# Last attention sums, turned rows' tile, first w_sp loads and the difference's stores: other queues, pools and places in a transformer block

## The chip, the cores and the metric

One core of a Trainium2 chip. A core has five engines with instruction streams of their own: TensorE (PE; matmuls, PEld its weight loads), VectorE (DVE), ScalarE (ACT), GpSimd (POOL) and SyncE (SP, which here only issues DMAs). They meet through semaphores. The metric is the device time of one execution in microseconds (us), lower is better; "the time" is the median of three runs.

## The reference

A transformer block in fp32 on x of 2048 rows by 512:

```
h   = x + wo · MHA(LN(x))                 32 heads of 16, softmax over 2048 keys
z   = gelu(LN(h) · w_in)                  2048 x 1376, halves z1 and z2 of 688
g   = w_sp · LN(z2) + b_sp                w_sp is 2048 x 2048: it mixes rows
out = h + (z1 * g) · w_out
```

## The kernel before

All products of w_in, wo, w_sp and w_out are made in three parts (mm3, L109 to L111): each fp32 operand is split into a high and a low part, and high·high, high·low and low·high are summed in PSUM. A split is one ScalarE copy (high, L101) and one VectorE subtraction (low, L106); for w_sp's blocks the lines are L989 and L990.

Three stages matter here.

**Attention** (up to about 1352 us). Per group of heads and block of 512 queries, scores, exponentials and products with v, and a `gather` (L760ff.): ScalarE and VectorE copy the result from PSUM to the tile `o`; then for each of four heads SyncE stores the head's rows to `o_scr` (L775) and its sums of exponentials into the tile `sums` (L776). `more_h` makes the first three rows' h between the last units, normalizes and turns them (`flip`, which returns `write`: four DMAs to `ht_scr`, L667).

**Row blocks** (1354 to 1520 us; the loop that starts with `for k in range(NB)`). Sixteen blocks of 128 rows, in the order 0, 1, 2, 8, 9, 10, 3, 11, ... 15; "row k" is the k-th of them. For row k, TensorE makes h of row k+3 (L642, 12 matmuls; none from k = 13 on) and the products of w_in with the row's turned block, in three chunks of 12 matmuls (four chunks of 344 columns for row 15). ScalarE does the gelu of each chunk (L1054) and, after the first chunk, splits `o` of row k+4 and `ht`, the turned block of row k+1 (`split_turned`). VectorE takes statistics of the second half of z (L1114 to L692); ScalarE normalizes it (L1066) and stores both halves to `z_scr` from its own DMA queue (L1061, L1067). Then `meanwhile` issues on SyncE: the fetch of row k+2's turned block (`fetch_turned`, L675), loads for row k+6, and the writes of row k+3's turned block. From row 8 of the loop on, the two halves of the rows meet (rows k and k-8 by number) and VectorE or GpSimd forms t1, t2, t3 and n4 of them.

Also here the first blocks of w_sp are fetched and combined: the w_sp product is made by a scheme of fewer block products, which needs `a22`, `s3` (a difference, L1009), `s2` and others. At the end of rows 11 and 12 `ask` loads a21, a22 and a11 (two DMAs of 256 KB each, L995); in row 13 GpSimd makes the six operations of `difference` and `sums`, and `sums` stores the difference to `s_scr` (two DMAs, L1031). In row 14 s3 is split, at its end s2, behind row 15 a22.

**The g products** (from 1520 us): products of w_sp's blocks, 48 matmuls each, the first two with s3 (with t3) and a22 (with n4), in two pools of PSUM banks; then the rest up to the output.

In the second and third stage the order on all five engines is that of the program text (`manual_schedule`). PSUM has eight banks. The w_in products rotate through seven of them (`mid_ps`), and h's product has the eighth. Each DMA of SyncE or ScalarE signals through one of eight completion semaphores (DMAHW0 to DMAHW7), taken in rotation by both; an issue waits until the transfer that used its semaphore before has landed. Tiles lie where pools are opened; a pool opened after another was closed lies on its memory, and then the first write waits for the last readers of the old tiles. The z tiles (`mid_2`) lie, among others, on attention's last `o` tile.

Of the kernel before, what the change touches and what calls it, by code (L numbers as in the profile page):

```python
# [22 lines left out]
DH = 16  # L23
# [37 lines left out]
def block_kernel(ctx: ExitStack, tc: tile.TileContext, x, wqkv, wo, w_in, w_sp4, b_sp, w_out, out):  # L61
# [648 lines left out]
    with ExitStack() as at:  # L710
# [49 lines left out]
        def gather(hg, qb, pool=sm):  # L760

            o = pp.tile([P, 512], F32, name="o", bufs=1)
            if pool is sm and not later:
                nc.scalar.activation(o, pv[0], AF.Copy)
            else:
                nc.vector.tensor_copy(o[:, :256], pv[0][:, :256])
                if later and pool is sm:
                    nc.vector.tensor_copy(o[:, 256:], pv[0][:, 256:])
                else:
                    nc.scalar.activation(o[:, 256:], pv[0][:, 256:], AF.Copy)  # L770
            cols = slice(qb * 512, (qb + 1) * 512)
            sums = pool.tile([P, 16], F32, name="sums")
            for j in range(4):
                h = head(hg, j % 2, j // 2)
                nc.sync.dma_start(o_scr[h * DH:(h + 1) * DH, cols], o[32 * j:32 * j + DH, :])  # L775
                nc.sync.dma_start(sums[32 * j:32 * j + 32, :], o[32 * j + DH:32 * j + VW, :])  # L776
            sums_[0] = (hg, cols, sums, pool)

        def by_age(place):
# [113 lines left out]
        def more_h(k):  # L893

            for _ in range(k):
                if not pieces:
                    sb = h_rows[made[0] // (3 * DB)]
                    acc = later[0].tile([P, 512], F32, name="h")
                    pieces.extend([sb, acc, h_products(sb, acc)])
                sb, acc, products = pieces  # L900
                next(products)
                made[0] += 1
                if made[0] % (3 * DB):
                    continue
                pieces.clear()
                if made[0] == 6 * DB:
                    split_turned(h_rows[0])
                after = h_rows[made[0] // (3 * DB)]
                o = os_.pop(after)
                hi, lo = o2s[after] = [e2.tile([P, DB, P], F32R, name=f"o2{i}", bufs=1) for i in range(2)]  # L910
                nc.vector.tensor_copy(hi, o)
                add_h(sb, acc, lambda: nc.vector.tensor_sub(lo, o, hi.bitcast(F32)))
                mv, rs = scale_h(sb)
                hn = e2.tile([P, D], F32, name="hn", bufs=3)
                nc.vector.tensor_scalar(hn, xrs.pop(sb), mv[:, 0:1], rs,
                                        op0=ALU.subtract, op1=ALU.mult)
                flip(sb, hn)()

        made = [0]
        units = [(hg, qb, kb) for hg in range(HG) for qb in range(NQ) for kb in range(NB)]  # L920
        turn, later = [0], []
# [2 lines left out]
        with tc.manual_schedule(engines={E.PE, E.Activation, E.DVE, E.SP}):  # L924
            end = len(units) - 2 * LEAD
            for n in range(0, end, 2):
                hg, qb, kb = units[n]
                if hg + 1 < HG and n % 64 < 24 and n % 4 == 0:
                    load_k(hg + 1, [n % 64 // 4])
                if hg + 1 < HG and n % 64 < 12 and n % 4 == 2:  # L930
                    load_d(hg + 1, [n % 64 // 4])
                if hg + 1 < HG and n % 64 == 30:
                    load_v(hg + 1)
                if kb == 2 and n // NB + 3 < HG * NQ:
                    load_q(n // NB + 3)
                place = n % NB // 2
                while m < min(8 * HG * NQ, n // 2 + LEAD + 1 + (not place and n > 0)):
                    for kind, some in max_pair(m, True).items():
                        steps_of[kind].extend(some)
                    m += 1  # L940
                if place or not n:
                    if place != 1 or n == 2:
                        play(START if not n else BEFORE if n + 2 == end else LAST if place == 7 else ORDER, units[n:n + 2])
                else:
                    play(FIRST_TWO, units[n:n + 4])
                if kb == 6 and sums_:
                    invert()
                if n % 32 == 16 and n < 6 * 32:
                    load_weights(n // 32)
                if n in (476, 482):  # L950
                    load_o(h_rows[(476, 482).index(n)])
                if n == 482:
                    split_o(h_rows[0], "pool", "pool")
            load_o(h_rows[2])
            hT.append(wc.tile([P, 2, 2, DB, P], F32R, name="hT", tag="w2"))
            maxima.close()
            for stack in reversed(singles):
                stack.close()
            doubles.extend(at.enter_context(tc.tile_pool(name=f"ps_d{i}", bufs=1, space=PSUM)) for i in range(2))
            later.append(attn.enter_context(tc.tile_pool(name="ps_l", bufs=1, space=PSUM, side="right")))  # L960
            play_final(units[end:])
    attn.close()


# [24 lines left out]
            nc.scalar.activation(hi, src, AF.Copy)  # L989
        (nc.gpsimd if el == "pool" else nc.vector).tensor_sub(lo, src, hi.bitcast(F32))  # L990

    def load_a(halves, i, j, p):

        for n, t in enumerate(halves):
            nc.sync.dma_start(t, w_sp4[p + HB * i][:, HB * j + QB * n:HB * j + QB * n + QB, :])  # L995

    def cut(t):
        return [t[:, QB * n:QB * n + QB, :] for n in range(2)]
# [12 lines left out]
    def half(name, tag, bufs=2, pool=None):  # L1011
        return [(pool or e2).tile([P, QB, P], F32, name=name, tag=tag, bufs=bufs) for _ in range(2)]

    def ask(i, j, p, tag, pool=None):

        t = half(f"a{i}{j}", tag, 3 if tag in ("xr", "hn") else 2, pool)
        load_a(t, i, j, p)
        return t

    def difference(a11, a21, e=nc.vector):  # L1020
# [5 lines left out]
    def sums(p, a11, a21, a22, e=nc.vector):  # L1026

        combine(e, a21, a21, a22, ALU.add)
        combine(e, a11, a21, a11, ALU.subtract)
        for n in range(2):  # L1030
            nc.sync.dma_start(cut(s_scr[p])[n], a11[n])  # L1031

    ctx.enter_context(tc.manual_schedule(engines={E.PE, E.Activation, E.DVE, E.Pool, E.SP}))
    with ExitStack() as mid:
        m2 = mid.enter_context(tc.tile_pool(name="mid_2", bufs=2))
        zs, zst = {}, {}
        ph = mid.enter_context(tc.tile_pool(name="mid_ph", bufs=1, space=PSUM))
        ps = mid.enter_context(tc.tile_pool(name="mid_ps", bufs=7, space=PSUM))

        def new_z(sb):  # L1040
            zs[sb] = [m2.tile([P, FH], F32, name=f"z{i}", bufs=1 + 4 * i) for i in range(2)]
# [49 lines left out]
        for k in range(NB):  # L1091
# [5 lines left out]
                nb = minus_mean(e2, mv, rs)  # L1097
            if k == NB - 3:
                s3 = difference(a11, a21, nc.gpsimd)
                sums(0, a11, a21, a22, nc.gpsimd)  # L1100
            if k == NB - 2:
                ops = {"s3": put(w[0], s3)}
            if k == NB - 1:
# [18 lines left out]

            def meanwhile():
                if k + 2 < NB:
                    fetch_turned(row[k + 2], m2)
                if k + 6 < NB:
                    load_o(row[k + 6])
                if new is not None:
                    write()

            gate_z(sb, meanwhile)
            if not k:
                invert()
            if k == NB - 5:
                a21, a22 = ask(1, 0, 0, "rc"), ask(1, 1, 0, "o")
            if k == NB - 4:
                a11 = ask(0, 0, 0, "xr")
            if k == NB - 2:
                ops["s2"] = put(w[1], a11)
        ops["a22"] = put(w[2], a22)  # L1140
# [3 lines left out]
    with ExitStack() as fin:  # L1144
# [41 lines left out]
        for p in range(HB):  # L1186
# [18 lines left out]
            if not last:  # L1205
# [7 lines left out]
                nxt["s3"] = put(new[0], difference(a11, a21))  # L1213
                if not p:
                    close67()
                sums(p + 1, a11, a21, a22)
                nxt["s2"] = put(new[1], a11)
            else:
                a11 = put(f[0], a11)
# [269 lines left out]
```

## Time and profile before

| what | us |
|---|---|
| median of three runs | 1810.49 (1808.0 to 1813.44) |
| profiled execution | 1808.73 |
| its span | 1807.0 |
| TensorE busy | 1789.6 |
| VectorE, ScalarE, GpSimd busy | 1519.9, 1376.2, 222.3 |

A row of a timeline reads: start, duration, engine, line, operation, out<-in, shape, count, and in brackets the idle time of the engine before it with what ended it. A row of the waits reads: who waited for whom, then total, number and longest. A row of the chain reads: start, duration, what. "SPq" and "ACTq" are DMA issues on SyncE's and ScalarE's queue.

### The profile page before, as it was taken

To read this page: it belongs to the slowest core of one execution; us is meant where nothing else is said; L and a number is where in the kernel's file an instruction comes from. 1 tells how busy PE (TensorE), PEld (TensorE's weight loads), DVE (VectorE), ACT (ScalarE), POOL (GpSimd) and SP (SyncE) were. 2 spreads that over 40 slices of the span, in tenths; PEclk is the share of its full clock that TensorE was granted. 3 is DMA by queue.
4 is the path that set the end of the run, shared out by engine and by line. 5 is a ranking of instruction groups with operands and counts; after the bars stand their busy time and mean duration, and the time that the engine had idled before them with its cause. 6 is when DMAs were issued, how large, how long until landed. Compare 5 with 4: busy or idle time off the path is not lost.

```text
span 1807.0 us, 35997 instructions
## 1 busy us (share of the span) xinstructions
PE 1789.6 (99%) x13307; PEld 1046.6 (58%) x13307; DVE 1519.9 (84%) x3051; ACT 1376.2 (76%) x2673; POOL 222.3 (12%) x299
## 2 busy tenths in 40 slices
PE   9999999999999999999999999999999998999999
PEld 6876444444444444444444444444448887999998
DVE  6487999999999999999999999999847886778664
ACT  3224999999999999999999999999984444334231
POOL 2241000011010100000000000000100863001111
PEclk9999999999999999999999999999999999999999
DMA  5687211221131121122022121110247775668562
GB/s 197 180 197 191 45 28 34 48 58 35 39 61 33 42 44 28 24 58 34 17 50 37 26 40 36 28 21 15 63 103 196 218 205 161 215 203 278 185 196 92
DMA packets 251608, 169.86 MB, mean 94 GB/s; under 512 B 158264, under 2 KB 196680, under 8 KB 250088
## 3 DMA queue, kind: packets, MB, share of 16 engines
q1 hardware_dynamic: 246648, 156.15, 33.9%
q10 hardware_dynamic: 4752, 11.41, 1.7%
q8 instruction: 105, 1.72, 0.4%
q14 instruction: 71, 0.58, 0.1%
q0 software_dynamic: 32, 0.01, 0.0%
HBM read 103.88 MB, written 62.69 MB: 92 GB/s over the span
## 4 chain that ended last, share of the span: by engine, by line
PE 97%; DMA 1%; DVE 1%; SPq 0%; ACT 0%; POOL 0%; issue 0%; ACTq 0%; DVEq 0%; POOLq 0%
PE pv L754 30%; PE s L728 11%; PE s L238 9%; PE m L728 9%; PE m L238 7%; PE acc L109 5%; PE acc L111 5%; PE acc L110 5%; PE g L111 4%; PE g L110 4%; PE g L109 4%; PE acc L642 2%; PE tp L1349 1%; PE h L642 1%; PE acc L1370 0%; PE tp L392 0%
## 5 line engine op out<-in xcount | busy, mean ns | idle before, releaser
L732 ACT ACTIVATE pt<-s 128x512 f32<-128x512 f32 (+1 forms) x1149 | 668.7, 633 | 3.3 <-PE s L728 1.7
L754 PE MATMUL pv<-pt,vst 128*32 128x256 f32 (+1 forms) x6048 | 595.2, 467 | 0.0
L243 DVE TENSOR_REDUCE mx<-s 128x1 f32<-128x512 f32 x826 | 540.4, 684 | 42.1 <-PE s L238 33.9
L732 ACT ACTIVATE pt<-m 128x512 f32<-128x512 f32 x855 | 500.6, 616 | 0.2 <-PE m L728 0.2
L243 DVE TENSOR_REDUCE mx<-m 128x1 f32<-128x512 f32 x682 | 453.0, 683 | 28.2 <-PE m L238 22.5
L728 PE MATMUL s<-qst,kst 50*128 50x512 f32 x1193 | 418.6, 438 | 0.0
L238 PE MATMUL s<-kst,qst 48*128 48x512 f32 x963 | 343.9, 422 | 0.0
L728 PE MATMUL m<-qst,kst 50*128 50x512 f32 x855 | 340.1, 440 | 0.0
L238 PE MATMUL m<-kst,qst 48*128 48x512 f32 x794 | 291.2, 423 | 0.0
L728 PEld LDWEIGHTS s<-qst,kst 50*128 50x128 f32 x1193 | 187.6, 184 | 144.9 <-DVE mx L243 91.0
L754 PEld LDWEIGHTS pv<-pt,vst 128*32 128x32 f32 x6048 | 120.5, 108 | 217.2 <-issue 208.1
L728 PEld LDWEIGHTS m<-qst,kst 50*128 50x128 f32 x855 | 146.4, 184 | 129.4 <-DVE mx L243 88.9
L238 PEld LDWEIGHTS s<-kst,qst 48*128 48x128 f32 x963 | 166.9, 185 | 40.3 <-issue 12.8
L238 PEld LDWEIGHTS m<-kst,qst 48*128 48x128 f32 x794 | 137.2, 185 | 41.6 <-issue 15.5
L103 POOL CAST mparts<-nm 128x16 fp32r<-128x16 f32 x32 | 6.3, 196 | 865.5 <-DVE nm L256 865.5
L248 ACT ACTIVATE ab<-s 128x512 f32<-128x512 f32 x167 | 100.3, 601 | 14.2
L252 DVE CUSTOM_DVE_ANT_0 ab<-s,ab 128x512 f32<-128x512 f32 x137 | 93.5, 683 | 5.1 <-PE s L238 5.1
L989 ACT ACTIVATE ws<-a 128x512 fp32r<-128x512 f32 x80 | 45.7, 620 | 48.7 <-PE g L111 23.8
L252 DVE CUSTOM_DVE_ANT_0 ab<-m,ab 128x512 f32<-128x512 f32 x112 | 76.5, 683 | 4.8 <-PE m L238 4.8
L109 PE MATMUL acc<-wi,hT 128*128 128x464 f32 (+2 forms) x196 | 72.7, 371 | 7.2 <-ACT hT L101 7.2
L238 PE MATMUL s<-dst,qst 48*128 48x512 f32 x167 | 79.7, 477 | 0.0
L111 PE MATMUL acc<-wi,hT 128*128 128x464 f32 (+2 forms) x196 | 72.8, 371 | 0.0
(219 smaller groups left out, 2554.6 us busy)
## 6 DMA issues: line engine op xcount, KB each, us to landing
a<-in_w_sp SPq DMA_DIRECT2D x80, 256.0 KB
qst<-q_scr SPq DMA_DIRECT2D x192, 64.0 KB
z_scr<-z ACTq DMA_DIRECT2D x32, 344.0 KB
kst<-k_scr SPq DMA_DIRECT2D x42, 256.0 KB
k_scr<-part SPq DMA_DIRECT2D x16, 512.0 KB
q_scr<-part SPq DMA_DIRECT2D x16, 512.0 KB
z<-z_scr SPq DMA_DIRECT2D x14, 344.0 KB
b<-z_scr SPq DMA_DIRECT2D x24, 172.0 KB
```

The costliest lines, as they stand in the source:

```text
L109: nc.tensor.matmul(ps, lh, rh, start=first, stop=False)
L110: nc.tensor.matmul(ps, lh, rl, start=False, stop=False)
L111: nc.tensor.matmul(ps, ll, rh, start=False, stop=last)
L238: nc.tensor.matmul(acc, q[r, p, c], keys[r, p], start=True, stop=True)
L243: nc.vector.reduce_max(at(t, e if t else e - 1), acc, axis=AX.X)
L248: nc.scalar.activation(ab[0], acc, AF.Relu)
L252: nc.vector.tensor_tensor_reduce(ab[0], acc, ab[0], 1.0, LOW, ALU.add, ALU.max, at(0, 0))
L642: yield nc.tensor.matmul(acc, o2[b][:, d, :], wo2[a][:, d, :], start=i == 0, stop=i == 3 * DB - 1)
L728: nc.tensor.matmul(out, kst[hg % 2][r, p, kb * P:(kb + 1) * P], qst[hg * NQ + qb][r, p, :], start=True, stop=True)
L732: nc.scalar.activation(out, scores, AF.Exp, scale=DH ** -0.5)
L754: nc.tensor.matmul(pv[0][32 * j:32 * j + 32, cols], vst[hg % 2][:, c:c + 32], pt[:, places[t, p], cols], start=kb == 0, stop=kb == NB - 1 ...
L989: nc.scalar.activation(hi, src, AF.Copy)
```

## The change

Five edits. The last `gather` loads its sums from ScalarE's queue. The third row's turned block is written behind the last gather's stores (`writes`). Turned blocks have a pool of their own, `mid_3`, in place of `mid_2`. a21, a22 and a11 of the first product are loaded from ScalarE's queue. The stores of the difference to `s_scr` are issued at the end of row 13's `meanwhile`, behind the fetch of row 15's block. And `mid_ps` has five banks, on the right side of PSUM.

```diff
@@ gather
                 nc.sync.dma_start(o_scr[h * DH:(h + 1) * DH, cols], o[32 * j:32 * j + DH, :])
-                nc.sync.dma_start(sums[32 * j:32 * j + 32, :], o[32 * j + DH:32 * j + VW, :])
+                e = nc.scalar if pool is not sm else nc.sync
+                e.dma_start(sums[32 * j:32 * j + 32, :], o[32 * j + DH:32 * j + VW, :])
@@ more_h
-                flip(sb, hn)()
-
+                writes.append(flip(sb, hn))
+                if made[0] < 9 * DB:
+                    writes.pop()()
+
+        writes = []
...
             play_final(units[end:])
+            writes.pop()()
@@ load_a, ask
-    def load_a(halves, i, j, p):
+    def load_a(halves, i, j, p, e=nc.sync):
         for n, t in enumerate(halves):
-            nc.sync.dma_start(t, w_sp4[p + HB * i][:, HB * j + QB * n:HB * j + QB * n + QB, :])
+            e.dma_start(t, w_sp4[p + HB * i][:, HB * j + QB * n:HB * j + QB * n + QB, :])
...
-    def ask(i, j, p, tag, pool=None):
+    def ask(i, j, p, tag, pool=None, e=nc.sync):
         t = half(f"a{i}{j}", tag, 3 if tag in ("xr", "hn") else 2, pool)
-        load_a(t, i, j, p)
+        load_a(t, i, j, p, e)
@@ sums
-        for n in range(2):
-            nc.sync.dma_start(cut(s_scr[p])[n], a11[n])
+
+        def store():
+            for n in range(2):
+                nc.sync.dma_start(cut(s_scr[p])[n], a11[n])
+
+        return store
@@ the row blocks
-        ps = mid.enter_context(tc.tile_pool(name="mid_ps", bufs=7, space=PSUM))
+        ps = mid.enter_context(tc.tile_pool(name="mid_ps", bufs=5, space=PSUM, side="right"))
+        m3 = mid.enter_context(tc.tile_pool(name="mid_3", bufs=2))
...
-                sums(0, a11, a21, a22, nc.gpsimd)
+                store_s2 = sums(0, a11, a21, a22, nc.gpsimd)
...
-                    fetch_turned(row[k + 2], m2)
+                    fetch_turned(row[k + 2], m3)
                 if k + 6 < NB:
                     load_o(row[k + 6])
                 if new is not None:
                     write()
+                if k == NB - 3:
+                    store_s2()
...
-                a21, a22 = ask(1, 0, 0, "rc"), ask(1, 1, 0, "o")
+                a21, a22 = ask(1, 0, 0, "rc", e=nc.scalar), ask(1, 1, 0, "o", e=nc.scalar)
             if k == NB - 4:
-                a11 = ask(0, 0, 0, "xr")
+                a11 = ask(0, 0, 0, "xr", e=nc.scalar)
@@ the later products
-                sums(p + 1, a11, a21, a22)
+                sums(p + 1, a11, a21, a22)()
```

Three places of the instruction order. Lines of the changed program are numbered a few higher (L1054 is L1064, L995 is L1000, L1031 is L1038). In brackets stands what an instruction waits for, by semaphore: an engine's, or a DMA's.

ScalarE, from attention's last copy of `o` to row block 0, before:

```order
L770 ACTIVATE o<-pv 128x256 [waits DMAHW4_49,DMAHW3_49,DMAHW5_49,DMAHW2_49,DMAHW6_49,DMAHW1_49,DMAHW7_49,DMAHW0_49,DVE_49]
L1054 ACT_TABLE_LOAD [waits DMAHW3_49,DMAHW4_49,DMAHW2_49,DMAHW5_49,DMAHW1_49,DMAHW6_49,DMAHW0_49,DMAHW7_49,PE_49]
L1054 ACTIVATE z_19146<-acc 128x464 [waits Activation_49]
L101 ACTIVATE o_19162<-o 128x512 [waits Pool_49]
L101 ACTIVATE hT<-ht 128x512
```

and in the change:

```order
L770 ACTIVATE o<-pv 128x256 [waits DMAHW4_49,DMAHW3_49,DMAHW5_49,DMAHW2_49,DMAHW6_49,DMAHW1_49,DMAHW7_49,DMAHW0_49,DVE_49]
L777 DMA sums<-o 32x1x16 [waits DMAHW4_49,Activation_49,Pool_49]
L777 DMA sums<-o 32x1x16 [waits DMAHW6_49]
L777 DMA sums<-o 32x1x16 [waits DMAHW0_49]
L777 DMA sums<-o 32x1x16 [waits DMAHW1_49]
L1064 ACT_TABLE_LOAD
L1064 ACTIVATE z_19149<-acc 128x464 [waits PE_49]
L101 ACTIVATE o_19165<-o 128x512 [waits Pool_49]
L101 ACTIVATE hT<-ht 128x512 [waits DMAHW7_49]
```

The four loads of the sums stand between the copy and the first gelu's table load, and that load no longer waits for DMAs.

SyncE, from row 11's end to row 13's (`a` are blocks of w_sp, `hz` a turned row), before:

```order
L995 DMA a_20685<-in_w_sp 128x512 [waits DMAHW6_49]
L995 DMA a_20686<-in_w_sp 128x512 [waits DMAHW7_49,Activation_49]
L654 DMA h_scr<-xr 128x512 [waits DMAHW0_49,DVE_49]
L675 DMA ht<-ht_scr 128x4x128 [waits DMAHW2_49,DMAHW1_49,Activation_49]
L667 DMA ht_scr<-hz 32x16x32 [waits DVE_49]
L667 DMA ht_scr<-hz 32x16x32 [waits DMAHW3_49]
L667 DMA ht_scr<-hz 32x16x32 [waits DMAHW4_49]
L667 DMA ht_scr<-hz 32x16x32 [waits DMAHW6_49]
L995 DMA a_20803<-in_w_sp 128x512 [waits DMAHW7_49]
L995 DMA a_20804<-in_w_sp 128x512 [waits DMAHW1_49,Activation_49]
L1031 DMA s_scr<-a_20803 128x512 [waits DMAHW2_49,Pool_49]
L1031 DMA s_scr<-a_20804 128x512 [waits DMAHW3_49,Pool_49]
```

The next row there is the fetch of row 15's block. In the change:

```order
L654 DMA h_scr<-xr 128x512 [waits DMAHW7_49,DVE_49]
L675 DMA ht<-ht_scr 128x4x128 [waits DMAHW4_49,DMAHW2_49,DMAHW5_49,DMAHW0_49,Activation_49]
L667 DMA ht_scr<-hz 32x16x32 [waits DVE_49]
L667 DMA ht_scr<-hz 32x16x32
L667 DMA ht_scr<-hz 32x16x32 [waits DMAHW6_49]
L667 DMA ht_scr<-hz 32x16x32 [waits DMAHW0_49]
L675 DMA ht<-ht_scr 128x4x128 [waits DMAHW4_49,DMAHW2_49,DMAHW6_49,DMAHW0_49,Activation_49]
L1038 DMA s_scr<-a_20806 128x512 [waits DMAHW3_49,Pool_49]
L1038 DMA s_scr<-a_20807 128x512 [waits Pool_49]
```

The fetch of row 15's block follows its own four writes, and the two stores stand behind it.

ScalarE, from row 12's last gelu to row 13's second, in the change:

```order
L1064 ACTIVATE z_20726<-acc 128x464 [waits PE_49]
L1071 DMA z_scr<-z_20726 128x688 [waits DMAHW6_49,Activation_49]
L1076 ACTIVATE z_20727<-z_20727,nb,rs_r_20794 128x688 [waits DVE_49]
L1077 DMA z_scr<-z_20727 128x688 [waits DMAHW1_49,Activation_49]
L1000 DMA a_20806<-in_w_sp 128x512 [waits DMAHW3_49]
L1000 DMA a_20807<-in_w_sp 128x512 [waits DMAHW5_49]
L1064 ACTIVATE z_20819<-acc 128x464 [waits PE_49,Pool_49]
L101 ACTIVATE hT<-ht 128x512 [waits DMAHW0_49]
```

The two loads of a11 stand between row 12's second z store and row 13's first gelu, where there was nothing; the four of a21 and a22 stand likewise one row earlier.

## The prediction

> **What bounds the kernel now.** I read the page's busy table first, then the waits of TensorE (columns: total us, times, longest), then a table by stretch, then the chain of waits and each engine's timeline around the two long waits.
>
> ```profile
> PE 1789.6 (99%) x13307; PEld 1046.6 (58%) x13307; DVE 1519.9 (84%) x3051; ACT 1376.2 (76%) x2673; POOL 222.3 (12%) x299
> ```
>
> ```profile
> PE acc L109 <- ACT hT L101: 7.2, 1, 7.2
> PE acc L642 <- ACT o L101: 2.0, 1, 2.0
> ```
>
> TensorE sets the end, so an edit is worth what it takes out of TensorE's idle time or adds to it. The change issues the same products. These two idle stretches, and one of 0.6 us below, lie where it moves things. The granted clock is a second cost, seen in the table by stretch (span; busy times and counts of PE, PEld, DVE, ACT, POOL; clock, DMA share, GB/s):
>
> ```profile
> 1354.65:1367.39 12.74, 10.78 (x49) 8.86 (x48) 6.35 (x19) 4.52 (x8) 0.00 (x0) 1.00 0.39 97
> 1367.39:1377.64 10.25, 10.25 (x49) 9.03 (x48) 9.24 (x33) 4.55 (x9) 1.30 (x1) 1.00 0.97 245
> 1487.60:1495.07 7.47, 7.47 (x38) 6.76 (x36) 1.97 (x9) 3.16 (x6) 2.25 (x3) 1.00 0.85 245
> ...
> 1509.95:1520.29 10.34, 9.74 (x49) 9.21 (x49) 7.64 (x26) 4.61 (x10) 5.64 (x8) 0.81 0.41 144
> 1520.29:1527.90 7.61, 7.61 (x49) 7.61 (x50) 5.92 (x12) 4.84 (x9) 0.00 (x0) 1.00 0.32 103
> ```
>
> The rows are row blocks 0, 1, 13 and 15 and the first g product. Behind the 7.2 us of idle, the last row's 48 matmuls took 10.34 us at clock 0.81; the 48 of the same size after them took 7.6 at 1.00. In row block 0, with 2.0 us of idle, the clock stayed 1.00. [...]
>
> **Place A: from attention into the row blocks.** TensorE's and ScalarE's timeline, then four pieces of the chain:
>
> ```profile
> 1364.27 3.29 PE L642 MATMUL acc<-wo,o 128*128 128x512 f32 x12 [1.96 <-ACT o L101]
> 1353.25 0.38 ACT L770 ACTIVATE o<-pv 128x256 f32<-128x256 f32 x1 [2.54 <-DVE o L766]
> 1361.84 1.28 ACT L1054 ACT_TABLE_LOAD   x1 [8.21 <-DMA sums<-o]
> ```
>
> ```profile
> 1357.20 1.69 SPq L775
> ...
> 1358.93 0.51 SPq L776
> ...
> 1363.14 0.56 ACT z L1054
> 1363.69 0.53 ACT o L101
> ```
>
> Row block 0 takes 12.74 us, row block 1 10.25: **2.49 us** lost. ScalarE stood 8.21 us before its first gelu: the z tile that it writes lies where attention's last `o` tile lay, free only when the last of eight DMAs that read `o`, issued one behind another by SyncE, has landed.
>
> With a pool of their own for the turned rows z no longer lies on `o`; the order listing shows no DMA left in that table load's wait. ScalarE now issues the four sums itself: from 1353.63 on, four at SyncE's 0.51 to 0.58 end by 1355.9. Table load 1.28: 1357.2, just when the first chunk's 12 products (0.21 each from 1354.65) end. Then gelu 0.56, split of `o` 0.53 and VectorE's half, 0.7: about 1359.1. TensorE wants it at 1362.3: 3.2 us of slack and no wait. If all four issues took the 1.69 of the slowest SyncE row, 4.5 us would be added and 1.3 stay lost. I take 0, the other SyncE issues being near 0.5, and keep 1.3 for the range.
>
> **Place B: the last row's turned block.** Timelines of TensorE, SyncE and GpSimd:
>
> ```profile
> 1509.95 0.65 PE L109 MATMUL acc<-wi,hT 128*128 128x344 f32 x1 [7.23 <-ACT hT L101]
> 1493.88 0.98 SPq L995 DMA_DIRECT2D a<-in_w_sp  x2
> 1504.82 1.55 SPq L1031 DMA_DIRECT2D s_scr<-a  x2
> 1506.53 0.37 SPq L675 DMA_DIRECT2D ht<-ht_scr  x1
> 1497.38 1.29 POOL L1009 TENSOR_TENSOR s<-a,a 128x512 f32<-128x512 f32 x1 [7.38 <-DMA a<-in_w_sp]
> 1500.13 5.88 POOL L1009 TENSOR_TENSOR a<-a,a 128x512 f32<-128x512 f32 x4
> ```
>
> Row 14 began at 1495.07 and takes 7.47 like row 13, so row 15 was due at 1502.54 and came at 1509.95: **7.41 us**. The fetch of its block stands on SyncE behind the difference's two stores; these wait for GpSimd's six operations, and GpSimd for the last two `a` loads, which SyncE issued at 1493.88. Then comes the slow clock, with an idle 0.6 (10.34 − 9.74) before the first g product: 10.34 − 7.59 = **2.75 us**. That 0.6 is a wait for the last gelu, which reads a bank that g takes over; with five banks on the other side the order shows g's first wait without ScalarE.
>
> In the change the stores stand behind the fetch, and the six loads are on ScalarE. The fetch needs row 15's four block writes on SyncE, the third of which waits for the completion slot of ScalarE's z store:
>
> ```profile
> 1486.62 0.71 DVE L661 STREAM_TRANSPOSE hz<-hn 128x512 f32<-128x512 f32 x1
> 1488.38 0.33 ACTq L1061 DMA_DIRECT2D z_scr<-z  x1
> 1490.44 0.33 ACTq L1067 DMA_DIRECT2D z_scr<-z  x1
> 1491.21 2.76 DMA ht<-ht_scr
> SPq L667 <- DMA z_scr<-z: 21.1, 5, 5.5
> ```
>
> Source ready at 1487.33; z store landed at 1491.2 (row 14's fetch waited for the same one); two more issues of 0.5, a landing of 2.8, the fetch with its own 2.8: the block is there at about 1498, or with the longest such wait (5.5 from 1488.4 on) at 1500.5. ScalarE meanwhile splits s3 and can split row 15 from about 1499.9, so its half is ready by 1500.5, at worst 1501.1, before 1502.54. VectorE's half is closer:
>
> ```profile
> 1494.66 0.69 DVE L106 TENSOR_TENSOR hT<-ht,hT 128x512 fp32r<-128x512 f32 x1 [5.25 <-ACT hT L101]
> ...
> 1500.50 3.18 DVE L990 TENSOR_TENSOR ws<-s,ws 128x512 fp32r<-128x512 f32 x2 [2.06 <-ACT ws L989]
> ...
> 1515.83 1.29 DVE L990 TENSOR_TENSOR ws<-a,ws 128x512 fp32r<-128x512 f32 x2 [2.07 <-ACT ws L989]
> ```
>
> A pair of splits took 1.29, or 3.18 beside GpSimd's additions. That puts row 15's low half at 1501.1 or 1502.7, wanted at 1503.0 (TensorE's third matmul); were it pushed by both, 0.8 late. I take 0.
>
> ScalarE's added issues: two at 1490.8 delay its next gelu by about 1 us, four fall before row 12's first gelu:
>
> ```profile
> 1482.85 0.56 ACT L1054 ACTIVATE z<-acc 128x464 f32<-128x464 f32 x1 [2.15 <-PE acc L111]
> ...
> 1493.99 0.63 ACT L101 ACTIVATE hT<-ht 128x512 fp32r<-128x512 f32 x1 [2.57 <-DMA ht<-ht_scr]
> ```
>
> Both times ScalarE had more than 2 us of idle time at hand, so I cost them at nothing; without that cover, 1 to 2 us. [...]
>
> **What is late next.** TensorE now reaches the first g product at 1502.54 + 7.59 = 1510.1 and the second, which needs the split of a22, at 1517.7 (the low half at 1518.0). Before, it got there at 1527.88:
>
> ```profile
> 1527.88 0.32 PE L109 MATMUL g<-n,ws 128*128 128x344 f32 x1
> 1495.27 0.93 DVE L1114 BATCH_NORM_STATS2 zst<-z 128x6 f32<-128x344 f32 x2
> 1498.22 0.21 DVE L692 TENSOR_SCALAR nb<-rs_r,zmv 128x1 f32<-128x1 f32 x1
> 1515.16 1.15 ACT L989 ACTIVATE ws<-a 128x512 fp32r<-128x512 f32 x2 [0.40 <-POOL n L987]
> 1516.22 0.79 ACT L1054 ACTIVATE z<-acc 128x344 f32<-128x344 f32 x2
> 1519.99 0.21 DVE L692 TENSOR_SCALAR nb<-rs_r,zmv 128x1 f32<-128x1 f32 x1
> 1525.66 2.50 DVE L990 TENSOR_TENSOR ws<-a,ws 128x512 fp32r<-128x512 f32 x4
> ```
>
> The a22 split ends a chain over VectorE and ScalarE that does not shrink: from row 15's low half on, statistics 3.16 (1495.27 to 1498.43), normalization and its store about 1.3, s2's split 1.15, gelus 0.79, statistics 3.16, then 6.3 to a22's first low half (1519.99 to 1526.3): 15.9 us. From 1501.1 it ends at 1517.0, from 1502.7 at 1518.6, and with s2's pair slow too (+1.9) at 1520.4. Against 1518.0: a new wait of 0, 0.6 or 2.4 us. I take **1.2**, between the upper two, since any other delay on these engines only adds. That is below the 2.0 us behind which the clock held.
>
> **The rest** costs nothing. Five banks instead of seven: a bank comes round five chunks on; the closest case is row 15's last chunk at 1508, whose bank was read by a gelu done by 1501.5. The third row's writes now go out behind the eight `o` DMAs; its fetch lands near 1363 and is wanted at 1369. The rotation of completion slots is shifted for three rows:
>
> ```profile
> ACT hT L101 <- DMA ht<-ht_scr: 10.4, 2, 7.8
> SPq L675 <- DMA z_scr<-z: 4.7, 1, 4.7
> ```
>
> Of all rows only 14 and 15 made ScalarE wait for a block, so the early rows have room, at a DMA share of up to 0.97 too. From 1520.29 on TensorE did not idle, so what is saved is kept as long as later loads keep their lead.
>
> **Sum.** 2.49 + 7.41 + 2.75 − 1.2 = 11.45 us off the profiled 1808.73: 1797.3. The runs' median, 1810.49, lies 1.8 above: **1799.0**. Bounds: a gain of 12.65 with no new wait; 12.65 − 2.4 − 1.2 = 9.05 with the slow values (of 1.3 and 0.8 only the larger, about): 1797.8 to 1801.4, and with the scatter of the runs (−2.5, +3) 1795 to 1804.
>
> **Rivals.**
>
> 1. *Row 15's block is still late.* The loads go out beside z stores and writes at a DMA share of 0.85. For: z stores held SyncE up to 5.5 us. Against: 2 us of slack, and the loads start earlier. With the block 3 to 5 us late and the clock slow again, B gives about 3.5, A its 2.5: gain 6, **1804.5**. Chance 0.12.
> 2. *TensorE runs into VectorE's chain.* If the second product waits 4 us and its clock drops (2.2 more), the gain is 12.65 − 6.2 = 6.5: **1804.0**. It decides once that wait passes a point between 2.0 and 7.2. For: VectorE is 84% busy. Against: 1.6 us above my worst sum. 0.08.
> 3. *The change does not do what it says.* ScalarE's four sums have waits for slots that SyncE's transfers hold, so A's wait may stay; B's fetch, moved forward, still waits for its own writes. Gain under 5.4: **1807**. Against: those slots belong to transfers long landed. 0.06.
> 4. *Slower.* The shifted rotation puts each row's fetch on a slot held by the same row's z store, as once in the trace (4.7 us, row 14). That delay left row 14 just in time: split at 1493.99 + 0.6, wanted 1495.07. So it decides beyond some 5 us a row. At 7.2, each of 12 rows loses 2.2: 26 − 12 = +14, **1824**. Against: the order has the old slots back from the fourth row on. 0.04.
>
> **Chances.** The forecast has 0.70. Measurements of this kernel tell 0.3% (5.4 us) from no change, so faster means below 1805.1: 0.70, half of rival 1 (0.06) and most of rival 2 (0.07) make 0.83. The same: 0.06 + 0.01 + 0.06 = 0.13. Slower: 0.04. The range 1795 to 1806 holds the forecast and rivals 1 and 2.
>
> **What would show it.** In the changed profile: no wait of `acc` L642 on `o`, row block 0 as long as row block 1; no wait of `acc` L109 on `hT`, or one under 1 us; the last row's 48 matmuls at clock 1.00 in 7.6 us; a new wait of the second g product on `ws` of 0 to 2.4 us. Wrong would be a row-15 wait of 3 us or more, a second slow clock, or repeated waits on `hT` in the middle rows.

## The result

The changed kernel takes 1798.31 us (median of four runs, 1798.14 to 1800.21), the kernel before, with the run taken beside it, 1810.26 (1808.0 to 1813.44): a ratio of 0.9935, 95% interval 0.9918 to 0.9952. That is 12.0 us, or 0.65%, less; the forecast was 1799.0. The profiled execution of the change, 1800.21 us with a span of 1798.4, happens to be the longest of the four; a second profile of the same kernel (the run `ctl` below, span 1796.1) is nearer to the others.

TensorE's waits, first in the changed kernel's profile, then in the second profile of the same kernel (total us, times, longest):

```profile
PE acc L111 <- DVE hT L106: 2.1, 1, 2.1
PE acc L465 <- DVE idle L462: 1.2, 1, 1.2
```

```profile
PE acc L111 <- DVE hT L106: 0.7, 1, 0.7
PE g L109 <- ACT ws L994: 0.6, 1, 0.6
```

The waits of 7.2 us on row 15's turned block and of 2.0 us on `o` are gone. In their place stands a shorter wait on VectorE's half of row 15's split and, in the second profile, one on the split of a22. (The wait at L465 was there before.)

The table by stretch shows where the time went. Columns: span; busy times and counts of PE, PEld, DVE, ACT, POOL; granted clock, DMA share, GB/s. The changed kernel, row blocks 0 and 1 (here from h's first matmul on), row 15, and the 48 matmuls behind it:

```profile
1352.12:1362.46 10.34, 10.34 (x52) 9.12 (x49) 8.01 (x21) 4.57 (x8) 1.29 (x1) 1.00 0.44 104
1362.46:1372.71 10.25, 10.25 (x50) 9.01 (x49) 8.63 (x27) 4.43 (x8) 1.30 (x1) 1.00 0.76 207
...
1500.37:1511.83 11.46, 9.35 (x50) 9.06 (x48) 8.90 (x22) 3.82 (x7) 11.00 (x13) 0.85 0.59 199
1511.83:1519.36 7.53, 7.53 (x51) 7.53 (x49) 6.26 (x16) 5.12 (x10) 1.24 (x2) 1.00 0.25 96
```

and the same kernel's second profile, row 14, row 15 and the 48 matmuls:

```profile
1492.25:1499.73 7.48, 7.48 (x37) 6.76 (x36) 5.13 (x12) 4.13 (x8) 6.67 (x5) 1.00 0.48 151
1499.73:1508.23 8.50, 7.81 (x50) 7.53 (x48) 6.12 (x16) 3.71 (x7) 8.26 (x9) 1.00 0.72 240
1508.23:1516.49 8.26, 7.69 (x51) 7.40 (x49) 6.69 (x19) 3.78 (x8) 4.00 (x6) 1.00 0.31 117
```

Row block 0 is as long as row block 1 (10.34 and 10.25 us; from the same h matmul on it was 12.49 before, 1351.78 to 1364.27). Row 15 now follows row 14 at once, but its first low-half product stands: in the first profile for 2.12 us with a slow clock behind (0.85), so that 48 matmuls took 11.46 us; in the second for 0.69 us at full clock, 8.50.

Two corrections to the words ahead of the prediction. The change has six edits, not five. And the 48 g matmuls that were called the first product are two products of 24, s3 with t3 and s2 with t2; the "second product", a22 with n4, is the third. Their times and their order stay as told.

SyncE's timeline at the place where the fetch stood behind the stores, in the changed kernel:

```profile
1487.21 2.68 SPq L667 DMA_DIRECT2D ht_scr<-hz  x4
1494.72 0.38 SPq L675 DMA_DIRECT2D ht<-ht_scr  x1
1500.71 2.00 SPq L1038 DMA_DIRECT2D s_scr<-a  x2
```

The fetch goes out 6.0 us ahead of the stores; before, it went out 1.7 us behind them, at 1506.53.

TensorE reached the row blocks up to 1.9 us earlier or later from execution to execution. To compare kernels without that, I use one stretch of each trace: from the first h matmul of row block 0 to the first matmul of a22 with n4. Before, the change, and the change again:

```profile
1351.78:1527.88 176.10, 166.32 (x796) 147.23 (x793) 132.30 (x379) 73.26 (x134) 92.22 (x101) 0.98 0.68 192
```

```profile
1352.12:1519.36 167.24, 165.12 (x797) 147.37 (x793) 134.89 (x378) 73.33 (x134) 93.51 (x101) 0.99 0.71 203
```

```profile
1351.44:1516.49 165.05, 163.79 (x797) 145.66 (x793) 132.73 (x376) 71.92 (x132) 93.69 (x101) 1.00 0.72 205
```

The stretch falls from 176.10 to 167.24 and 165.05 us. What lies behind it to the end of the span is 279.12 before and 279.04 and 279.61 after: all the gain is in this stretch. Below, "the stretch" is this one.

### The profile page after: what moved, and what is told of

It is laid out like the page before. It is cut to its first block, busy times and chain, and to the rows that moved or that the text cites. A ratio compares the mean times of both kernels' runs of the same rounds, so it can differ in the third digit from the quotient of the medians.

```text
span 1798.4 us, 36014 instructions
## 1 busy us (share of the span) xinstructions
PE 1788.7 (99%) x13307; PEld 1046.0 (58%) x13307; DVE 1523.9 (85%) x3051; ACT 1376.6 (77%) x2673; POOL 223.8 (12%) x299
## 4 chain that ended last, share of the span: by engine, by line
PE 98%; DVE 1%; DMA 0%; ACT 0%; issue 0%; SPq 0%; ACTq 0%; DVEq 0%
PE pv L754 30%; PE s L728 11%; PE s L238 9%; PE m L728 9%; PE m L238 7%; PE acc L109 6%; PE acc L111 5%; PE acc L110 5%; PE g L111 4%; PE g L110 4%; PE g L109 4%; PE acc L642 2%; PE tp L1361 1%; PE h L642 1%; PE acc L1382 0%; PE tp L392 0%
## 5 line engine op out<-in xcount | busy, mean ns | idle before, releaser
L111 PE MATMUL acc<-wi,hT 128*128 128x464 f32 (+2 forms) x196 | 72.7, 371 | 2.1 <-DVE hT L106 2.1
L1064 ACT ACTIVATE z<-acc 128x464 f32<-128x464 f32 (+2 forms) x64 | 27.5, 456 | 60.0 <-PE acc L111 47.2
```

The source lines that it names most:

```text
L111: nc.tensor.matmul(ps, ll, rh, start=False, stop=last)
```

## The experiments

The first four take one edit alone on the kernel before; the others start from the change.

### One edit alone

**The pool.** Edit, on the kernel before:

```diff
+        m3 = mid.enter_context(tc.tile_pool(name="mid_3", bufs=2))
...
-                    fetch_turned(row[k + 2], m2)
+                    fetch_turned(row[k + 2], m3)
```

> The kernel before with one edit alone: the turned rows' tiles in a pool of their own (7 banks, sums still loaded by SyncE). Theory (place): what held the first gelu is only that z lies on attention's last o tile; with another place the first gelu comes near 1357, TensorE's wait of 2.0 us on o goes, row block 0 falls from 12.74 to about 10.3 us, row 15's wait stays 7.2 and the time falls by about 2.5 us. Rival (queue): the eight issues on one queue are the trouble, the o split waits for them anyway, and row block 0 stays above 12 us.

Measured: 1807.36 us, 0.9987 of before (0.9977 to 0.9996). Row block 0 took 10.34 us, with no wait on `o`; row 15 waited 7.4. The first gelu's table load waited for TensorE's first chunk alone:

```profile
1357.62 1.28 ACT L1055 ACT_TABLE_LOAD   x1 [3.66 <-PE acc L111]
```

So the place of z accounts for all of place A, with the eight issues still on SyncE. The time is 2.7 us less, as expected.

**The sums on ScalarE's queue.** The kernel before with this edit of the change, and no other:

```diff
-                nc.sync.dma_start(sums[32 * j:32 * j + 32, :], o[32 * j + DH:32 * j + VW, :])
+                e = nc.scalar if pool is not sm else nc.sync
+                e.dma_start(sums[32 * j:32 * j + 32, :], o[32 * j + DH:32 * j + VW, :])
```

> The kernel before with one edit alone: the last four sums loaded from ScalarE's queue; z still lies on the o tile. Theory (place, with 3.2 us of slack): the eight DMAs go out on two queues by about 1356.3 and land near 1358, the gelu follows at 1359.3, the split of o ends near 1361, and row block 0 is about 10.3 us long too: this edit alone also gives the 2.5 us. Rival: the four landings on ScalarE's path come too late (after 1360), and 1 us or more of the 2.0 us wait stays.

Measured: 1808.39 us, 0.9993 (0.9983 to 1.0002): the times do not tell it from no change. A wait of 0.37 us on `o` stayed:

```profile
1360.92 1.28 ACT L1055 ACT_TABLE_LOAD   x1 [6.54 <-DMA o_scr<-o]
```

The sums were off the path, but the four stores of `o`, still read from under z, landed at 1360.9, 2.9 us later than I had put them. Row block 0 took 10.9 us (12.49 before, 10.34 with the pool): this edit alone gives most of place A, not all. The stretch did not shrink (176.47 us), since row 15's wait was 8.8 us in this execution.

**The stores behind the fetch.** On the kernel before, loads on SyncE; `sums` returns `store` as in the change, and:

```diff
-                sums(0, a11, a21, a22, nc.gpsimd)
+                store_s2 = sums(0, a11, a21, a22, nc.gpsimd)
...
                     write()
+                if k == NB - 3:
+                    store_s2()
```

> The kernel before with one edit alone: the difference's two stores behind the fetch of row 15's block; the six loads stay on SyncE. Theory (order of the stores decides B): the fetch goes out near 1495.5 and lands near 1498.3, but GpSimd works from 1497.4 to 1506 as before, so VectorE's split pair of s3 takes 3.2 and its half of row 15 ends near 1505: TensorE's wait falls from 7.2 to about 2.5 us (on VectorE's hT), gain 5 us and up to 2 more of clock. Rival (late loads): with the loads late the block gains little, the wait stays 4 us or more.

Measured: 1804.0 us, 0.997 (0.9961 to 0.9979); the stretch 171.42 us. The wait on ScalarE's `hT` was gone, and one of 1.71 us on VectorE's stood there (2.5 expected), with 0.59 and 0.69 us ahead of the g products:

```profile
1506.28 0.42 PE L111 MATMUL acc<-wi,hT 128*128 128x344 f32 x1 [1.71 <-DVE hT L106]
1514.37 0.40 PE L109 MATMUL g<-t,ws 128*128 128x344 f32 x1 [0.59 <-POOL t L987]
1522.82 0.43 PE L109 MATMUL g<-n,ws 128*128 128x344 f32 x1 [0.69 <-ACT ws L989]
```

The 0.59 us is the wait that stood there before, too; it goes only with the five banks (below), whatever releaser the profile names. The order of two stores is worth 6 us of the 12 by the times. The stretch of this profile shows less, because TensorE waited 2.18 us for `o` in row block 0 here and ran slow behind it.

**The loads on ScalarE's queue.** On the kernel before, the stores still ahead of the fetch:

```diff
-                a21, a22 = ask(1, 0, 0, "rc"), ask(1, 1, 0, "o")
+                a21, a22 = ask(1, 0, 0, "rc", e=nc.scalar), ask(1, 1, 0, "o", e=nc.scalar)
...
-                a11 = ask(0, 0, 0, "xr")
+                a11 = ask(0, 0, 0, "xr", e=nc.scalar)
```

> The kernel before with one edit alone: a21, a22, a11 loaded from ScalarE's queue; the stores still stand ahead of row 15's fetch. Theory (order of the stores): GpSimd starts some 3 us earlier (near 1494), ends near 1502, the fetch goes out near 1503 and lands near 1506: TensorE's wait is about 4.5 us, gain 2.7 us, clock still low behind it. Rival (late loads are the cause): wait under 2 us.

Measured: 1808.78 us, 0.9996 (0.9987 to 1.0005): no change that the times can tell. The trace does show one. TensorE's wait on `hT` was 5.3 us, 1.9 less than before, where I had 4.5. GpSimd started at 1497.13, about when it did before, but the rows ran later in this execution (row 14 began at 1496.63; before, at 1495.07), mostly because of a slow clock behind 1.68 us of idle time in row block 0. Counted from row 14's first matmul GpSimd was 1.8 us earlier, 0.5 instead of 2.3 us behind it (3 us expected). So late loads account for about 1.9 us of the 7.2; that they were the cause, with a wait under 2 us left, falls.

### Parts taken back from the change

**The changed kernel again**, unaltered:

> The changed kernel again, unaltered. In its first profile TensorE waited 2.12 us for VectorE's half of row 15 and then ran 11 matmuls at 0.43 to 0.49 us instead of 0.32. Theory (the clock's drop behind some 2 us of idle is a matter of phase, since 2.0 us before and 1.7 us in the run with the stores alone did not bring it and 1.7 and 2.2 us in row block 0 of two other runs did): the wait is again 1.8 to 2.4 us, the slow matmuls may be gone, and the median lies near 1798.3. Rival (2.1 us always brings it): the wait and the slow matmuls are both there.

Measured: 1798.57 us, 0.9938 (0.9921 to 0.9954). The median was as expected, the wait was not: 0.69 us. It varies from execution to execution, as the next paragraphs show; this execution does not tell whether 2.1 us always brings the slow clock, since it had no such wait.

**The loads back on SyncE.**

```diff
-                a21, a22 = ask(1, 0, 0, "rc", e=nc.scalar), ask(1, 1, 0, "o", e=nc.scalar)
+                a21, a22 = ask(1, 0, 0, "rc"), ask(1, 1, 0, "o")
...
-                a11 = ask(0, 0, 0, "xr", e=nc.scalar)
+                a11 = ask(0, 0, 0, "xr")
```

> The changed kernel with the six loads of a21, a22, a11 back on SyncE. Theory (the loads' move is worth little by itself but keeps GpSimd and what follows early): GpSimd's six operations start 3 to 5 us later, TensorE's wait on VectorE's hT stays about 2 us, and the first two g products wait 0.5 to 0.7 us each, as in the run with the stores alone; 1 to 3 us slower than the change. Rival (no part): same time within 0.5 us.

Measured: 1800.31 us, 0.9946 (0.9931 to 0.9961), 1.7 us above `ctl`; the stretch 167.64 against 165.05. GpSimd started 3.3 us later than in `ctl` (1496.31 and 1493.06, row 15 starting at 1500.54 and 1499.73), and the waits were these:

```profile
PE acc L111 <- DVE hT L106: 1.7, 1, 1.7
PE g L109 <- ACT ws L994: 1.4, 1, 1.4
```

The 1.4 us are on a22, more than the 0.5 to 0.7 expected; the first g product did not wait, as the five banks are in. So once the stores are out of the way the move of the loads is worth 1.7 us by the times (each of the four runs is longer than each of `ctl`'s). The stretch is 2.6 us longer than in `ctl`, but only 0.4 longer than in the first profile of the change, which had a slow clock. That the move acts through GpSimd and VectorE is read from these waits, and only the one on a22 is clear of the change's own: the wait on `hT` was 0.7 and 2.1 us in its two profiles.

**Seven banks**, on the left as before.

```diff
-        ps = mid.enter_context(tc.tile_pool(name="mid_ps", bufs=5, space=PSUM, side="right"))
+        ps = mid.enter_context(tc.tile_pool(name="mid_ps", bufs=7, space=PSUM))
```

> The changed kernel with seven banks for w_in on the left, as before. Theory (the last gelu holds the first g matmul by 0.6 us, but what comes next waits for VectorE and ScalarE anyway): the wait of 0.6 us before the first g matmul is back, the wait of 0.6 us on a22's split goes, and from the start of row 15 to the first matmul with n4 the time is the same within 0.3 us. Rival (0.6 us of its own): 0.6 us longer.

Measured: 1798.74 us, 0.9933 (0.9917 to 0.995), the same as the change. The first g matmul waited 0.59 us again, and the wait on a22 was gone:

```profile
PE acc L111 <- DVE hT L106: 0.9, 1, 0.9
...
PE g L109 <- POOL t L992: 0.6, 1, 0.6
```

The stretch was 165.31 us against 165.05, so the 0.6 us that the five banks save are handed on to the next wait, as the theory had it.

**The third row's write in its old place.**

```diff
-                writes.append(flip(sb, hn))
-                if made[0] < 9 * DB:
-                    writes.pop()()
+                flip(sb, hn)()
...
-            writes.pop()()
```

> The changed kernel with the third row's turned block written before the last gather's stores, as before. Theory (nothing waits for either): row block 0 stays at 10.3 to 10.4 us, no new wait of TensorE, same time within 0.3 us in the traces. Rival (the stores of o, some 2 us later, hold something in row blocks 0 to 3): a wait on o or hT there.

Measured: 1798.19 us, 0.9929 (0.9914 to 0.9944); row block 0 10.37 us, no wait there; the stretch 164.56 us, 0.5 less than in `ctl`, all of it in the wait of row 15 (0.22 for 0.69). The edit costs and gives nothing that these traces show.

**The sums back on SyncE.**

```diff
-                e = nc.scalar if pool is not sm else nc.sync
+                e = nc.sync
```

> The changed kernel with the last four sums loaded by SyncE again. Theory (the pool alone gives all of place A): row block 0 stays at 10.3 to 10.4 us, no wait on o; same time within 0.3 us in the traces. Rival (sums on ScalarE take part): the wait on o is back, up to 2 us.

Measured: 1798.2 us, 0.9928 (0.9914 to 0.9943); row block 0 10.36 us, no wait on `o`. With the pool in place the move of the sums is worth nothing. The stretch was 165.53 us because row 15 waited 1.70 us here.

### What is late next, and a version without it

**GpSimd's last four operations left out.** The edit, in `sums`:

```diff
-        combine(e, a21, a21, a22, ALU.add)
-        combine(e, a11, a21, a11, ALU.subtract)
+        if e is not nc.gpsimd:
+            combine(e, a21, a21, a22, ALU.add)
+            combine(e, a11, a21, a11, ALU.subtract)
```

> The changed kernel without GpSimd's last four operations in row 13 (L1014 on a: they are left out for the first product, so that part of the w_sp product is not computed). Theory (VectorE is slowed by GpSimd working beside it): the split pair of s3 falls from 3.36 to about 1.3 us, VectorE's half of row 15 from 1.74 to 0.69, TensorE's wait of 2.1 us goes, the clock stays 1.00, and the last row takes 7.6 us; then the second g product waits 0 to 0.5 us on a22. Gain 2 to 4 us. Rival (VectorE's own queue or data that come late): the pair stays above 2.5 us and the wait above 1.5.

Measured: 1796.84 us, 0.9928 (0.9914 to 0.9943). TensorE did not wait for row 15 at all, and the stretch was 163.82 us. The time is 1.7 us below `ctl`'s, a little under the 2 to 4 expected, and the intervals overlap. VectorE's half of row 15 took 0.95 us instead of 1.74:

```profile
1498.17 2.66 DVE L995 TENSOR_TENSOR ws<-s,ws 128x512 fp32r<-128x512 f32 x2 [2.07 <-ACT ws L994]
1500.76 0.95 DVE L106 TENSOR_TENSOR hT<-ht,hT 128x512 fp32r<-128x512 f32 x1
```

The pair of s3 still took 2.66 us and not 1.3: GpSimd went straight on to its next operations (from 1497.0 on), so VectorE was never alone. That half of the expectation missed (a pair above 2.5 us was the rival's sign), because the run did not leave GpSimd idle. The other half held: with less of GpSimd's work beside it VectorE is in time.

**The splits in another order.** Row 14's split of s3 moves from ahead of the row's products to behind its gate, s2's behind row 15's `bn_stats`, a22's into the last gate (`then` is the split of a22 there):

```diff
-            if k == NB - 2:
-                ops = {"s3": put(w[0], s3)}
...
                 nc.vector.bn_stats(zst[sb][:, c, :], zs[sb][1][:, c * FC:(c + 1) * FC])
+            if k == NB - 1:
+                ops["s2"] = put(w[1], a11)
...
             if k == NB - 2:
-                ops["s2"] = put(w[1], a11)
-        ops["a22"] = put(w[2], a22)
+                ops = {"s3": put(w[0], s3)}
...
             put_t("t3", b12)
+            then()
```

> The changed kernel with splits in another order at the end of the row blocks: row 15's turned block before s3 (s3 after row 14's gate), s2 after row 15's statistics, a22 between t3 and t2 of the last gate. Theory: VectorE's half of row 15 is ready near 1500.6 (slowed by GpSimd, 1.7 us), so TensorE's wait falls below 0.3 us, the clock holds, and the chain to a22 ends before TensorE needs it: last row 7.6 us, span 3 to 4 us below the profiled execution of the change, time near 1796. Rival: the chain to a22 or s3 is late instead, and the second or first g product waits 2 us or more: no gain.

Measured: 1797.2 us, 0.9929 (0.9914 to 0.9944). Row 15's 48 matmuls took 7.55 us and there was no wait on `hT`. The next products waited 0.29 and 0.44 us on the last blocks of t (8.82 us for 48 matmuls instead of 7.53), since s2's split, 1.99 us on VectorE, now stood between row 15's statistics and their use. The stretch was 164.63 us, 0.4 less than in `ctl`; the span, 1796.2 us, is 2.2 below that of the change's first profile, where 3 to 4 were expected.

**The same, with s2 behind the statistics and a22 between t2 and t1.** Against the change (`first` and `then` are the splits of s2 and a22 in the last gate):

```diff
             nb = minus_mean(m2, mv, rs)
+            first()
...
             put_t("t2", t2)
+            then()
...
-            if k == NB - 2:
-                ops = {"s3": put(w[0], s3)}
...
-            gate_z(sb, meanwhile)
+            gate_z(sb, meanwhile, *([split_s2, split_a22] if k == NB - 1 else []))
...
-                ops["s2"] = put(w[1], a11)
-        ops["a22"] = put(w[2], a22)
+                ops = {"s3": put(w[0], s3)}
```

> As the run with the splits in another order, but s2's split behind row 15's statistics (it held them by 2 us there) and a22's between t2 and t1. Theory: no wait of TensorE on hT or a22, and the waits of 0.3 and 0.4 us on t in the last block of the first g products fall below 0.3 us in all; from the start of row 15 to the first matmul with n4 15.2 to 15.6 us; 1 to 1.5 us below the unaltered change. Rival (s2 itself is late now): a wait of 0.5 us or more on s2's split in these products, no gain over the other order.

Measured: 1797.58 us, 0.9924 (0.9909 to 0.9939). In the trace nothing is left to wait for, from row 15 to a22:

```profile
1501.57:1516.65 15.08, 15.08 (x98) 15.08 (x96) 12.14 (x33) 8.45 (x16) 11.29 (x13) 1.00 0.60 197
1353.30:1516.65 163.35, 163.35 (x797) 145.82 (x793) 129.87 (x374) 71.78 (x131) 92.96 (x101) 1.00 0.74 207
```

Span and TensorE's busy time are equal in both rows. The stretch is 163.35 us, 1.7 less than in `ctl` and 12.75 less than before. The median is 1.0 us below that of `ctl`, and the intervals overlap: the trace shows the gain, the times do not resolve it.

## Why the prediction was right

The time, 1799.0 forecast and 1798.31 measured, came out of a sum whose parts can be checked one by one.

- **Place A, 2.49 us: right.** Row block 0 fell to the length of row block 1: from its h matmuls to those ahead of row 2 the traces have 23.10 us before (1351.78 to 1374.88) and 20.59 after (1352.12 to 1372.71), 2.51 less. The reason given first, the place of z, is the whole of it: the pool alone gives 10.34 us. That ScalarE would issue the sums itself, which the sum also worked through, turned out not to matter. The four issues took 2.55 us (2.3 expected), the table load followed at 1356.79 (1355.9).
- **Place B, 7.41 us: right, with luck in one step.** From the h matmuls ahead of row 2 to row 15's first matmul the traces have 135.07 us before (1374.88 to 1509.95) and 127.66 after (1372.71 to 1500.37), 7.41 less. The fetch went out at 1494.72 and the working had 1495, but the working's times are those of the old kernel, whose rows run 2.2 us later there. Counted from row 14's first matmul (1492.89; 1495.07 before) the fetch went out 1.8 us behind it, in the second profile 2.1, where the working had them together: the block's four writes, whose landing it waits for, held it until 4.8 us behind the end of their issue (3.8 in the second profile), not 2.8. The 2 us of slack that the working left covered this; ScalarE stood for the block in neither profile. The runs with one edit put most of the cause where the chain had it: the stores alone give 6 us, and the loads alone take 1.9 us off the wait.
- **The 2.75 us of slow clock and bank: right, near by luck.** The run without any wait (the last one) takes 12.75 us out of the stretch, against 12.65 from 2.49 + 7.41 + 2.75. The term was read from one execution: behind the same long wait the last row's 48 matmuls took 10.34 us there, but 11.15 in the profile with the pool alone, 10.67 with the sums alone and 11.23 with the loads alone, so it lies between 2.8 and 3.6 us.
- **The new wait, 1.2 us: near in one profile of two, and half wrong in place.** I put all of it on a22 and none on row 15's low half, which was to be at worst 0.8 us late. In the second profile it is 0.69 on the low half and 0.57 on a22, 1.26 in all; in the first, 2.12 on the low half and nothing on a22. That the 1.26 is near the 1.2 is luck: 1.2 was a middle value for a22 alone. The step that failed is the time at which VectorE has the low half, and it has two parts. The low half's own length was taken as 0.69 us; beside GpSimd it takes 1.74 to 1.78. And the chain ahead of it began late: ScalarE's half of row 15 started 5.8 us behind row 14's first matmul in the first profile and 5.0 in the second (1498.71 and 1497.24), where the working had 4.8 (1499.9). VectorE's timeline in the first profile:

```profile
1497.88 3.36 DVE L995 TENSOR_TENSOR ws<-s,ws 128x512 fp32r<-128x512 f32 x2 [2.08 <-ACT ws L994]
1501.16 1.74 DVE L106 TENSOR_TENSOR hT<-ht,hT 128x512 fp32r<-128x512 f32 x1
```

  The chain behind it was about as long as worked out (15.9): from 1502.90 to a22's first low half, near 1518.7, is 15.8 us, and 16.3 in the second profile.
- **The clock behind a wait of about 2 us: wrong.** "Below the 2.0 us behind which the clock held" drew a bound from one case. Row 15 of the first profile lost 11.46 − 7.55 − 2.12 = 1.8 us to a slow clock behind 2.12 us of idle time. That is the second slow clock that was named as a sign of being wrong. With the longer wait it is why the profiled execution is 1.7 us above the next of its four runs.
- **The rest at nothing: right, but for ScalarE's issues of the loads.** The third row's write and the five banks brought no wait of TensorE. The two issues of a11 behind row 12's second z store were to delay the next gelu by about 1 us, under the cover of a later wait of ScalarE for row 14's block (2.57 us). In the change that block is there in time, so the cover is gone, and ScalarE goes from the issues straight to the gelu and to row 14's split, with VectorE's statistics, ScalarE's normalization and s3's split behind them. In the first profile and in the second:

```profile
1488.98 1.83 ACTq L1000 DMA_DIRECT2D a<-in_w_sp  x2
1490.91 0.56 ACT L1064 ACTIVATE z<-acc 128x464 f32<-128x464 f32 x1 [2.37 <-PE acc L111]
1491.37 0.62 ACT L101 ACTIVATE hT<-ht 128x512 fp32r<-128x512 f32 x1
```

```profile
1488.11 1.24 ACTq L1000 DMA_DIRECT2D a<-in_w_sp  x2
1489.45 0.56 ACT L1064 ACTIVATE z<-acc 128x464 f32<-128x464 f32 x1 [1.75 <-issue]
```

  The gelu starts 0.1 us behind the issues in both; the products that it reads had ended near 1488.0 in the first, so the PE named there was long done. (For the normalization of row 13 in the first profile, at 1495.84, the profile names the landing of a z store; VectorE's `nb`, which it reads, ended at 1495.81, so it could not have started earlier.) The longer pair of issues stands in the profile with the longer wait. No run takes these issues out by themselves: with the loads back on SyncE, row 14's block is late instead.

Of the rivals the first (row 15's block still late, clock slow again) came nearest in the first profile, for another reason: the block was there, its split was not. The slower case did not show; no row in the middle waited.

By the times the pool (2.7 us), the stores (6.1) and the loads (1.7, taken back from the change) make 10.5 of the 12.0 us. The pool and the stores were not run together, so where the other 1.5 us belongs is open; part of it can be the slow clock that the single edits still had in their profiles.

## What to carry to other kernels

Look at what stands ahead of an urgent transfer in the same queue and what that waits for: here two stores, read back only from 1617.20 on, over 110 us later, waited for GpSimd, and a fetch behind them cost TensorE 7.4 us and its clock (0.81 in the last row); moving the loads that fed GpSimd took out only 1.9 us of that wait. When a stall is taken out, walk the chain of the next one with the durations that operations have beside their neighbours, not with the ones they have alone (here 1.74 us for VectorE's half of a split, not 0.69), and ask whether the idle time that covered an added cost is still there. And a tile's place in memory can be a wait: one pool more took out 2.5 us, and with it the move of the sums to another queue was worth nothing.

## What the runs showed of the hardware

**VectorE and GpSimd slowed each other.** A 128x512 GpSimd operation on two tiles took 1.29 us alone and up to 1.82 beside VectorE's subtractions; these took 0.69 alone and up to 1.79 beside it. GpSimd's four additions in the changed kernel, and in the run with the splits in another order (min, median, max in ns):

```profile
L1014 POOL TENSOR_TENSOR a<-a,a x4: 1294/1500/1741, 1496.4 to 1500.7; 128x512 f32<-128x512 f32 x4
```

```profile
L1014 POOL TENSOR_TENSOR a<-a,a x4: 1289/1292/1822, 1496.6 to 1500.8; 128x512 f32<-128x512 f32 x4
```

In the second, VectorE's half of row 15 (1499.03, 0.69 us) got through at full speed, and one GpSimd operation took 0.53 us longer. Statistics, which read one tile, took 0.92 to 0.93 for two in both. The slow case, 1.74, is 1.05 us above the fast one. By what the two engines slow each other the traces do not show; they show these durations.

**The clock dropped behind 1.68 us of idle time, and held behind 1.96.** All cases of these profiles between 1.6 and 2.2 us in the stages of the change:

| idle time of TensorE, us | where | slow matmuls behind it |
|---|---|---|
| 1.68 | loads alone, row block 0 | yes: clock 0.86, 48 matmuls in 12.18 us |
| 1.70 | sums back on SyncE, row 15 | no: clock 1.00 |
| 1.71 | stores alone, row 15 | no: matmuls of 0.32 us |
| 1.71 | loads back on SyncE, row 15 | no: clock 1.00 |
| 1.96 | before, row block 0 | no: clock 1.00, the same 48 in 10.61 us |
| 2.12 | the change, row 15 | yes: clock 0.85 |
| 2.18 | stores alone, row block 0 | yes: clock 0.86, the same 48 in 11.92 us |

In the changed kernel the slow matmuls (0.49 instead of 0.32 us) began only 0.9 us after work had resumed, and lasted 3.4 us:

```profile
1503.69 0.33 PE L109 MATMUL acc<-wi,hT 128*128 128x344 f32 x1
1503.84 0.46 PE L110 MATMUL acc<-wi,hT 128*128 128x344 f32 x1
...
1507.26 0.34 PE L110 MATMUL acc<-wi,hT 128*128 128x344 f32 x1
```

So the length of the idle time alone does not part these seven cases. What does is not shown: a matter of phase, as was expected ahead of `ctl`, was the author's estimate, and no run tried it by itself.
